# One matmul for the shared last query rows of a head pair, tails in one query block, and another order of the work

## The chip, the cores and the metric

One Trainium2 chip, one of its cores. The metric is the device time of one execution in microseconds, lower being better. Engines are named as in the profile: PE (TensorE), DVE (VectorE), ACT (ScalarE), POOL (GpSimd), and SP, the engine whose queue issues all DMAs of this kernel.

## What is computed

Attention with pooled queries, followed by a gated MLP with mixing along the sequence:

```python
# q, k, v: (4 batches, 8 heads, 1152, 64)
q_pool = q.reshape(B, H, 576, 2, D).mean(axis=3)
scores = q_pool @ k^T / sqrt(64);  scores -= max(scores, axis=-1)
attn = exp(scores) / (sum(exp(scores)) + 1e-9)
x = (attn @ v) with heads side by side              # (4, 576, 512)
h = gelu(x @ w_in);  u, v = halves of h             # 512 columns each
v = layernorm(v) * g_ln
v = w_sg @ v + b_sg                                 # mixing over 576 positions
out = x + (u * v) @ w_out
```

Inputs come as float32 and the weights and scores need more than half precision: the kernel splits most operands into a high and a low part of 16 bits and adds up the products.

## The kernel before, in words

The 32 heads are taken as 16 pairs p. A head has 576 pooled queries: four blocks of 128 rows and a last one of 64, the tail. Keys are 9 blocks of 128. For each pair:

- `load` (lines 338 to 352) brings in the raw keys, queries and values of two heads. POOL adds neighbouring queries (`pool`, lines 423 and 425), ACT and DVE make the high and low parts (`q_hi` L441, `q_lo` L445, `k_hi` L428, `k_lo` L431), and DMA transposes on SP write `q1` and `k1` (L449, L435). `k1` holds the high part of the keys in partitions 0 to 63 and the low part in 64 to 127; `q1` holds the high part of the queries twice. A plain DMA copies the upper half of `k1` into `k2` (L438).
- `maxima` (L499, L505) finds the largest score of each query row ahead of the real scores: per block of 128 query rows two matmuls of 512 key columns and one of 128, with a reduction on DVE after each bank. The rows are counted r = 0 to 8. r = 4 is the shared block: 64 tail rows of the first head in the lower half, 64 of the second in the upper half. Its queries are two zero-padded blocks of `q1` (4 and 5), one for each head, so each of its pieces takes two accumulating matmuls, one for each head's keys. After r = 4, and again after r = 8, DVE gathers the maxima (`done`, L529), POOL splits them (`split`, L535 to L537) into columns of `n2` beside the low parts of the queries, and a transpose DMA (`turn`, L540) writes `q2`. The first `turn` carries blocks 0 to 4, the second blocks 5 to 9.
- `attend` then goes over the key blocks j of head 0 and head 1. A main unit is two matmuls of 512 columns into a PSUM bank, `scores(0)` with `k1`, `q1` and `scores(1)` with `k2`, `q2` (L574), the exponential on ACT (L582), a high part on ACT (L588), a rest (L593) and matmuls with the values into `avp` (L602, or L609 for pairs 0 and 2, which keep float32). A tail unit does the same for the last 64 queries against several key blocks; it follows j = 4 and j = 8. The rest of a "kept" unit, half of the main units by `KEEP`, is made by DVE from PSUM; that of the others by POOL from SBUF. All `scores(0)` stay in program order (the marker `sseq`), and so do all matmuls into `avp`.

After 8 heads of a batch, `project` (through `unit`, L757) multiplies by `w_in`, and `gmlp` does the rest and stores. This work lies between the attention of the following batch; for the last batch it stands alone at the end.

Nothing of this is issued in the order of the code. Each step is given to `Schedule.add` with an engine, a duration, what it reads and writes, and a due time; `Schedule.run` simulates forwards and backwards `PASSES` times, shifts some due times by the seeds in `MOVES`, and the last forward run emits the instructions. An engine takes its instructions strictly in the order emitted. PSUM has 3 score banks (`S`), 3 banks `X`, 1 bank `M`, and `avp`. Maxima of pairs 4 and later use only `X`.

The wait on which much below rests, as the code has it:

```python
q1r = [f"q1{c}{hh}"] + ([f"q1{c}0"] if hh else [])
add("PE", ds, lambda: scores(0), r=[f"k1{c}{hh}", "clear"] + q1r, ...)
add("PE", ds, lambda: scores(1), r=[f"k2{c}{hh}", f"q2{c}{hh}", f"k2z{c}"], ...)
```

Of the kernel before, what the change touches and what calls it, by code (L numbers as in the profile page):

```python
# [222 lines left out]
def attention_gmlp_kernel(  # L223
# [57 lines left out]
    q2 = tiles(const, 2, [128, 10, 128], F16, "q2")  # L281
    mp = tiles(const, 2, [128, 9, 3], F32, "mp")
    qs = const.tile([128, 10, D], F32, name="qs")
    n1 = const.tile([128, 10, 2, D], F16, name="n1")
    n2 = const.tile([128, 10, 128], F16, name="n2")
# [87 lines left out]
    def scales(p, i, due):  # L373
# [36 lines left out]
        add("DVE", 0.64, power, r=[f"ps{p}{i}"], w=[st, f"pm{i}"], due=due, rel=[("x", "sc", p, i)])  # L410

    def prepare(p):
# [5 lines left out]
        for h in range(2):  # L418
            blk = slice(5 * h, 5 * h + 5)

            def pool(h=h):

                nc.gpsimd.tensor_tensor(out=qs[:, 6 * h:6 * h + 4, :], in0=qr[:, h, :, 0, :], in1=qr[:, h, :, 1, :], op=ALU.add)  # L423
                r = slice(64 * h, 64 * h + 64)
                nc.gpsimd.tensor_tensor(out=qs[r, 4 + h, :], in0=qe[r, 0, :], in1=qe[r, 1, :], op=ALU.add)
# [22 lines left out]
            def q_turn(blk=blk):  # L448
                nc.sync.dma_start_transpose(out=q1[c][:, blk], in_=n1[:, blk].rearrange("p i t d -> p (i t d)"))  # L449

            add("POOL", 0.97, pool, r=["qr"], w=[f"qs{h}"], due=t + lead("PL", p) + h)
            add("ACT", 0.72, q_hi, r=[f"qs{h}", sct], w=[f"n1{h}"], due=t + lead("QH", p) + h * HS[p > 0])
            add("SP", 0.7, q_turn, late=LATE[1] * (p > 0), issue=1.25, r=[f"n1{h}"], w=[f"q1{c}{h}"], due=t + lead("QH", p) + h * HS[p > 0])
# [4 lines left out]
            add("DVE", 0.46, q_lo, port=True, r=[f"qs{h}", sct, f"n1{h}"], w=[f"n2q{h}"], due=t + lead("QL", p) + h * HS[p > 0])  # L458
# [22 lines left out]
    def maxima(p):  # L481
# [5 lines left out]
        def rows(r):  # L487

            return ([(0, 4), (1, 5)], [0, 1]) if r == 4 else ([(0, r)], [0]) if r < 4 else ([(1, r + 1)], [1])

        def piece_of(group, j0, nj, g):
            nonlocal n
            r0, x = group[0][0], ("x", p, group[0][0], g)
# [16 lines left out]
            cols = w * sum(len(ops) for _, ops, _ in group)  # L510
            heads = sorted({h for _, _, hs in group for h in hs})
            add("PE", cols / 2400.0 + 0.003 * len(group), piece, r=[f"q1{c}{h}" for h in heads] + [f"k1{c}{h}" for h in heads], w=[x],
                due=due, acq=(x, where))
            add("DVE", w * len(group) / 960.0 + 0.07, top, r=[x], w=[f"mp{c}{a}{g}" for a, _, _ in group], due=due - 0.5, rel=[x])

        for r in range(9):
            ops, hs = rows(r)

            for g in range(2):
                piece_of([(r, ops, hs)], 4 * g, 4, g)  # L520
            if r in (3, 4, 8):
                piece_of([(a, *rows(a)) for a in {3: range(4), 4: (4,), 8: range(5, 9)}[r]], 8, 1, 2)
            if r in (4, 8):
                due = t + lead("X", p) + lead("XS", p) * n * 1.29 if p else -20 + n
                h = r // 8
                nm = nmx[h]

                def done(h=h, nm=nm):
# [725 lines left out]
```

## Time and profile before

| | |
|---|---|
| median of 3 runs | 638.8 us (638.28 to 639.22) |
| the profiled execution | 635.98 us, of which 634.2 us from first to last instruction |
| PE, DVE, ACT, POOL busy | 603.6, 528.5, 531.0, 380.8 us |
| granted TensorE clock, mean | 1.000 of 2.4 GHz |
| DMA | 71.49 MB, of the 16 engines' time 52% |

Busy time of PE runs from a matmul's start to its modelled end, and ends overlap with the starts of the next ones: a mean of one is longer than its share of the time. The warm-up matmuls at line 920 count as busy too. The time of an SP row is that of issuing a DMA; when it lands is a separate number.

### The profile page before, as it was taken

Reading aid. Unit: us, or ns where it says so; the run is one execution under the profiler, and the core shown is the slowest. Engines: PE = TensorE matmul, PEld = TensorE weight load, DVE = VectorE, ACT = ScalarE, POOL = GpSimd, SP = SyncE. Lnnn points to the kernel's source line nnn. Section 1 sums busy time; section 2 is a strip of 40 time slices with the busy share of each in tenths; the row PEclk is TensorE's granted clock in tenths of the full one; section 3 lists DMA queues with packets and bytes.
Section 4 is the critical chain, followed back from the end, with each engine's and each line's share of the span. In section 5 each row is a group of like instructions: output and inputs, shape, how many; then the busy total and the mean of one; then the engine's idle time right before and its main releaser. Section 6 shows DMA issues by size and latency. Waiting matters only on the chain.

```text
span 634.2 us, 18243 instructions
## 1 busy us (share of the span) xinstructions
PE 603.6 (95%) x7228; PEld 409.2 (65%) x7228; DVE 528.5 (83%) x1052; ACT 531.0 (84%) x987; POOL 380.8 (60%) x481
## 2 busy tenths in 40 slices
PE   5899899997999899999999999999999999999997
PEld 3387567864567566667566775676666775776755
DVE  4989899898989999999987999879998997753662
ACT  7478898799999989999999999798999988784420
POOL 8133375477556688855574677785475565962163
PEclk9999999999999999999999999999999999999999
DMA  9988961957655245568678334807772221141002
GB/s 262 236 209 217 185 135 39 198 121 121 129 115 121 61 79 133 111 136 177 114 160 181 35 51 94 154 24 193 132 170 52 68 41 20 12 84 36 26 1 74
DMA packets 129078, 71.49 MB, mean 113 GB/s; under 512 B 107424, under 2 KB 111520, under 8 KB 128864
## 3 DMA queue, kind: packets, MB, share of 16 engines
q1 hardware_dynamic: 128992, 70.33, 51.7%
q8 instruction: 56, 0.92, 0.6%
q14 instruction: 30, 0.25, 0.1%
HBM read 36.23 MB, written 4.72 MB: 65 GB/s over the span
## 4 chain that ended last, share of the span: by engine, by line
PE 64%; DVE 14%; ACT 5%; issue 1%; DMA 1%; POOL 0%; ACTq 0%; DVEq 0%; POOLq 0%
PE px L757 18%; PE s L574 14%; PE avp L602 13%; PE pm L757 7%; PE px L499 7%; DVE mp L505 5%; DVE f L593 2%; PE s L757 1%; ACT f L588 1%; PE avp L609 1%; ACT e L582 1%; DMA x<-in_moe_w_out_dram 1%; DVE n L445 1%; PE pm L857 1%; DVE dn L644 1%
## 5 line engine op out<-in xcount | busy, mean ns | idle before, releaser
L593 POOL TENSOR_TENSOR f<-e,f 128x512 f16<-128x512 f32 (+2 forms) x182 | 193.0, 1068 | 108.1 <-ACT f L588 93.0
L574 PE MATMUL s<-q,k 128*128 128x512 f16 (+1 forms) x1152 | 231.2, 286 | 12.8 <-ACT e L582 5.2
L505 DVE TENSOR_REDUCE mp<-px 128x1 f32<-128x512 f32 (+2 forms) x316 | 199.8, 663 | 18.1 <-PE px L499 16.2
L602 PEld LDWEIGHTS <-f 128*128 128x128 f16 x3780 | 150.4, 97 | 56.3 <-issue 10.6
L602 PE MATMUL avp<-va,f 128*128 128x65 f16 x3780 | 166.0, 193 | 1.5 <-POOL f L593 1.0
L582 ACT ACTIVATE e<-s 128x512 f32<-128x512 f32 (+2 forms) x226 | 124.9, 558 | 15.6 <-PE s L574 11.1
L499 PE MATMUL px<-k,q 128*128 128x512 f16 (+1 forms) x454 | 118.7, 325 | 2.1 <-DVE mp L505 1.6
L574 PEld LDWEIGHTS <-k 128*128 128x128 f16 x1152 | 82.6, 99 | 51.0 <-issue 15.6
L588 ACT ACTIVATE f<-e 128x512 f16<-128x512 f32 (+2 forms) x182 | 107.1, 591 | 4.5 <-issue 2.0
L593 DVE TENSOR_TENSOR f<-s,f 128x512 f16<-128x512 f32 x126 | 85.9, 682 | 22.7 <-ACT f L588 22.3
L582 ACT ACTIVATE s<-s 128x512 f32<-128x512 f32 x126 | 76.9, 611 | 8.1 <-PE s L574 7.5
L588 ACT ACTIVATE f<-s 128x512 f16<-128x512 f32 x126 | 77.4, 614 | 4.3 <-PE avp L602 2.4
L499 PEld LDWEIGHTS <-q 128*128 128x128 f16 x480 | 42.2, 99 | 27.0 <-issue 6.2
L609 PEld LDWEIGHTS avp<-va,e 128*128 128x128 f32 x360 | 46.1, 192 | 3.1
L609 PE MATMUL avp<-va,e 128*128 128x65 f32 x360 | 45.6, 270 | 0.0
L757 PE MATMUL px<-wsg,vz 128*128 128x512 f16 x168 | 43.6, 379 | 0.0
L423 POOL TENSOR_TENSOR qs<-qr 128x256 f32<-128x256 f32 x32 | 25.1, 786 | 22.3 <-DVE n L445 11.2
L757 PE MATMUL px<-wout_h,xg 128*128 128x512 f32 x100 | 38.2, 425 | 0.0
L757 PEld LDWEIGHTS <-win_h 128*128 128x128 f16 x320 | 30.0, 98 | 12.6 <-issue 1.0
L648 POOL TENSOR_TENSOR x<-a,dn 128x320 f32<-128x320 f32 x32 | 25.3, 789 | 17.2 <-DVE dn L645 13.2
L757 PE MATMUL px<-xt,win_h 128*128 128x288 f16 (+2 forms) x220 | 34.9, 262 | 0.0
L757 PEld LDWEIGHTS <-vz 128*128 128x128 f16 x224 | 20.5, 98 | 20.6 <-issue 0.4
(166 smaller groups left out, 1012.3 us busy)
## 6 DMA issues: line engine op xcount, KB each, us to landing
kr<-in_k_dram SPq DMA_DIRECT2D x16, 576.0 KB, 4.6
qr<-in_q_dram SPq DMA_DIRECT2D x16, 512.0 KB, 4.0
vr<-in_v_dram SPq DMA_DIRECT2D x14, 576.0 KB, 4.1
k<-k SPq DMA_DIRECT2D x32, 144.0 KB, 3.1
x<-in_moe_w_in_dram SPq DMA_DIRECT2D x8, 512.0 KB, 5.9
out_dram<-t SPq DMA_DIRECT2D x16, 256.0 KB, 2.3
x<-in_moe_w_out_dram SPq DMA_DIRECT2D x8, 256.0 KB, 3.5
u<-in_moe_w_sg_dram SPq DMA_DIRECT2D x1, 1152.0 KB, 7.0
```

The costliest lines, as they stand in the source:

```text
L423: nc.gpsimd.tensor_tensor(out=qs[:, 6 * h:6 * h + 4, :], in0=qr[:, h, :, 0, :], in1=qr[:, h, :, 1, :], op=ALU.add)
L445: nc.vector.scalar_tensor_tensor(out=n2[:, blk, 0:D], in0=qs[:, blk], scalar=s[:, 1:2], in1=n1[:, blk, 0, :], op0=ALU.mult, op1=ALU.subtract)
L499: nc.tensor.matmul(out=bank(x)[:, w * i:w * i + w], lhsT=q1[c][:, o, :], rhs=k1[c][:, h, j0:j0 + nj, :].rearrange("p j k -> p (j k)"), sta ...
L505: nc.vector.tensor_reduce(out=mp[c][:, r0:r0 + len(group), g], in_=src, axis=AX.X, op=ALU.max)
L574: nc.tensor.matmul(out=buf(("s", u))[:, col:col + w], lhsT=kk[c][:, hh, j, :], rhs=qq[:, o:o + w], start=(i == 0 and m == 0), stop=(i == 1 ...
L582: nc.scalar.activation(out=s if kept else buf(("e", u))[:, 0:n], in_=s, func=AF.Exp, scale=SCALE * 2.0**-ASH)
L588: nc.scalar.activation(out=buf(("f", u))[:, 0, 0:n], in_=exponentials(), func=AF.Copy)
L593: eng.tensor_tensor(out=f[:, 1, 0:n], in0=exponentials(), in1=f[:, 0, 0:n], op=ALU.subtract)
L602: nc.tensor.matmul(out=avp[:, o:o + m], lhsT=w[:, col:col + 128], rhs=vv, start=(j == 0 and k == 0 and not tail and x == 0), stop=(j == KJ ...
L609: nc.tensor.matmul(out=avp[:, o:o + D + 1], lhsT=e[:, col:col + 128], rhs=vw[c][:, KJ * hh + j, :], start=(j == 0 and k == 0 and not tail) ...
L648: nc.gpsimd.tensor_tensor(out=xbuf[b % 2][:, :, col], in0=a[:, :, 0:D], in1=d.rearrange("p (i o) -> p i o", o=1).to_broadcast([128, 5, D]) ...
L757: nc.tensor.matmul(out=bank(m)[:, o[0] if o else slice(0, cols)], lhsT=l, rhs=r, start=(k + j == 0), stop=(k + j == n - 1), skip_group_che ...
```

## The change

The shared block r = 4 becomes one matmul per piece. A tenth block of `n1` gets the first head's tail queries in the first 64 columns of the first 64 rows and the second head's in the other corner, zeros elsewhere; after the transpose that is a block-diagonal query block (`q1` block 9). A new tile `kx` holds the high parts of both heads' keys, one above the other; two new DMAs per pair copy them from `k1`. The product has the high parts of the keys alone, for the maxima of these 128 rows. Tail queries of both heads now lie in one block 4, which belongs to the second half of each step: POOL adds them in one instruction of 128 rows, the first half has blocks 0 to 3, the second blocks 4 to 8 (9 for `q1`). The first `done`/`split`/`turn` now comes after r = 3. The tail units of both heads read the second half's `q1` and `q2`.

Beside that: `KEEP` goes from 0.5 to 0.53, first chunks of `project` wait for `wn0`, `wn1`, and in the last batch its first three units use only banks `X` and `M` and wait for the last maxima, the others for the last head's output; planner durations, `PASSES` and `MOVES` are new, so the whole order is.

```diff
-    q2 = tiles(const, 2, [128, 10, 128], F16, "q2")
+    q2 = tiles(const, 2, [128, 9, 128], F16, "q2")
+    kx = const.tile([128, KJ, 128], F16, name="kx")
...
-            blk = slice(5 * h, 5 * h + 5)
+            blk = slice(4, 9) if h else slice(0, 4)
+            n = 4 + h
...
-                nc.gpsimd.tensor_tensor(out=qs[:, 6 * h:6 * h + 4, :], in0=qr[:, h, :, 0, :], in1=qr[:, h, :, 1, :], op=ALU.add)
-                r = slice(64 * h, 64 * h + 64)
-                nc.gpsimd.tensor_tensor(out=qs[r, 4 + h, :], in0=qe[r, 0, :], in1=qe[r, 1, :], op=ALU.add)
+                nc.gpsimd.tensor_tensor(out=qs[:, 5 * h:5 * h + 4, :], in0=qr[:, h, :, 0, :], in1=qr[:, h, :, 1, :], op=ALU.add)
+                if h:
+                    nc.gpsimd.tensor_tensor(out=qs[:, 4, :], in0=qe[:, 0, :], in1=qe[:, 1, :], op=ALU.add)
+
+            def q_cross():
+
+                for a in range(2):
+                    r = slice(64 * a, 64 * a + 64)
+                    nc.gpsimd.tensor_copy(n1[r, 9, a, :], n1[r, 4, a, :])
+
+            def k_cross(h=h):
+                nc.sync.dma_start(out=kx[64 * h:64 * h + 64], in_=k1[c][0:64, h])
...
-            def q_turn(blk=blk):
+            def q_turn(blk=slice(4, 10) if h else blk):
                 nc.sync.dma_start_transpose(out=q1[c][:, blk], in_=n1[:, blk].rearrange("p i t d -> p (i t d)"))
...
-            return ([(0, 4), (1, 5)], [0, 1]) if r == 4 else ([(0, r)], [0]) if r < 4 else ([(1, r + 1)], [1])
+            if r == 4:
+                return q1[c][:, 9, :], kx, [f"q1{c}1", "kx0", "kx1"]
+            return q1[c][:, r, :], k1[c][:, r // 4 if r < 4 else 1], [f"q1{c}{r // 5}", f"k1{c}{r // 5}"]
...
-                for i, (_, ops, _) in enumerate(group):
-                    for k, (h, o) in enumerate(ops):
-                        nc.tensor.matmul(out=bank(x)[:, w * i:w * i + w], lhsT=q1[c][:, o, :],
-                                         rhs=k1[c][:, h, j0:j0 + nj, :].rearrange("p j k -> p (j k)"), start=(k == 0),
-                                         stop=(k == len(ops) - 1))
+                for i, r in enumerate(group):
+                    qb, kb, _ = rows(r)
+                    nc.tensor.matmul(out=bank(x)[:, w * i:w * i + w], lhsT=qb, rhs=kb[:, j0:j0 + nj, :].rearrange("p j k -> p (j k)"),
+                                     start=True, stop=True)
...
-            if r in (4, 8):
+            if r in (3, 8):
...
-        o = (704 if hh else TM) if tail else 768 * hh
+        o = TM + TT * hh if tail else 640 * hh
+        qh = 1 if tail else hh
...
-        q1r = [f"q1{c}{hh}"] + ([f"q1{c}0"] if hh else [])
+        q1r = [f"q1{c}{qh}"]
...
-        add("PE", ds, lambda: scores(1), r=[f"k2{c}{hh}", f"q2{c}{hh}", f"k2z{c}"], w=[f"s{u}"], due=g - 0.7)
+        add("PE", ds, lambda: scores(1), r=[f"k2{c}{hh}", f"q2{c}{qh}", f"k2z{c}"], w=[f"s{u}"], due=g - 0.7)
...
-        ready = [f"xt{ct}" for ct in range(CT if b < B - 1 else CT - 1)]
+        last = b == B - 1
+        ready = ["wn0", "wn1"] + [f"xt{ct}" for ct in range(CT - last)]
+        early = ready + (["nm0", "nm1"] if last else [])
+        if last:
+            ready = ready + [f"x{b % 2}{H - 1}"]
...
-KEEP = (0.5, 0.5)
+KEEP = (0.53, 0.53)
...
-PASSES = 14
+PASSES = 7
```

`MOVES` goes from 76 seeds to 100 other ones.

## Rows read from the trace of the kernel before

**Rows 1.** The page, parts 1 and 4: busy time, and the last chain by engine.
```profile
PE 603.6 (95%) x7228; PEld 409.2 (65%) x7228; DVE 528.5 (83%) x1052; ACT 531.0 (84%) x987; POOL 380.8 (60%) x481
PE 64%; DVE 14%; ACT 5%; issue 1%; DMA 1%; POOL 0%; ACTq 0%; DVEq 0%; POOLq 0%
```

**Rows 2.** Three stretches: length, busy by engine (instructions), granted clock, DMA share, GB/s.
```profile
20.00:160.00 140.00, 128.62 (x1412) 94.05 (x1411) 129.03 (x271) 116.27 (x232) 70.76 (x100) 1.00 0.75 160
160.00:560.00 400.00, 393.46 (x5137) 261.22 (x5136) 354.79 (x692) 372.22 (x689) 267.80 (x331) 1.00 0.50 103
560.00:634.20 74.20, 70.13 (x625) 47.36 (x624) 34.19 (x63) 27.13 (x45) 28.96 (x28) 1.00 0.14 38
```

**Rows 3.** PE and weight loads in the first of these, for line 920 (warm-up) alone.
```profile
20.00:160.00 140.00, 7.45 (x22) 2.11 (x22) 1.00 0.75 160
```

**Rows 4.** PE in order of time: runs of maxima matmuls, four each (start, length, count).
```profile
520.98 1.03 PE L499 MATMUL px<-k,q 128*128 128x512 f16 x4
515.13 0.39 PE L499 MATMUL px<-k,q 128*128 128x128 f16 x4
```

**Rows 5.** Weight loads of the maxima, all pairs (count, ns min/median/max).
```profile
L499 PEld LDWEIGHTS <-q x480: 95/98/153, 18.2 to 552.2; 128*128 128x128 f16 x160
```

**Rows 6.** DVE, groups by line and shape (count, busy us, mean ns, idle before).
```profile
L505 DVE TENSOR_REDUCE mp<-px 128x1 f32<-128x512 f32 x271 | 177.0, 680 | 17.1 <-PE px L499 15.4 <-PE px L396 0.6
L593 DVE TENSOR_TENSOR f<-s,f 128x512 f16<-128x512 f32 x126 | 85.9, 682 | 22.7 <-ACT f L588 22.3
L445 DVE SCALAR_TENSOR_TENSOR n<-qs,sc,n 128x320 f16<-128x320 f32 x32 | 21.9, 691 | 0.6 <-DMA q<-n 0.4
```

**Rows 7.** POOL and ACT, the same view.
```profile
L593 POOL TENSOR_TENSOR f<-e,f 128x512 f16<-128x512 f32 x126 | 150.2, 1193 | 88.9 <-ACT f L588 75.9 <-PE s L574 3.3 <-PE px L499 3.2
L425 POOL TENSOR_TENSOR qs<-qe 64x64 f32<-64x64 f32 x32 | 11.4, 357 | 1.3
L536 POOL CAST n<-nm 128x5 f16<-128x5 f32 x32 | 7.6, 239 | 2.2
L441 ACT ACTIVATE n<-qs,sc 128x640 f16<-128x640 f32 x32 | 26.9, 841 | 2.0 <-POOL qs L425 2.0
```

**Rows 8.** DMA of line 438: all of them (KB, us to landing), and two issues on SP.
```profile
k<-k SPq DMA_DIRECT2D x32, 144.0 KB, 3.1
42.79 1.13 SPq L438 DMA_DIRECT2D k<-k  x2
```

**Rows 9.** Pair 0: first two reductions, second gathering, second `turn`, first tail's `scores(1)`.
```profile
18.99 1.28 DVE L505 TENSOR_REDUCE mp<-px 128x1 f32<-128x512 f32 x2
36.69 0.16 DVE L529 TENSOR_REDUCE nm<-mp 128x5 f32<-128x15 f32 x1
40.89 1.23 SPq L540 DMA_TRANSPOSE q<-n  x1
35.88 0.53 PE L574 MATMUL s<-q,k 128*128 128x64 f16 x6
```

**Rows 10.** Line 540, all `turn`s: from issue to landing.
```profile
DMA to landing us min/median/max: 2.6/2.9/6.9
```

**Rows 11.** Pair 15: its second `turn` and the first tail's `scores(1)`.
```profile
555.96 1.24 SPq L540 DMA_TRANSPOSE q<-n  x1
553.03 0.31 PE L574 MATMUL s<-q,k 128*128 128x64 f16 x5
```

**Rows 12.** Waits of PE (engine, line, for what: us, times, longest).
```profile
PE s L574 <- ACT e L582: 5.2, 12, 1.2
PE s L574 <- DVE f L593: 4.2, 8, 1.0
PE s L574 <- DMA q<-n: 2.5, 1, 2.5
```

**Rows 13.** The last head's end: ACT empties `avp`, POOL norms, ACT takes up `xn`.
```profile
578.92 0.44 ACT L641 ACTIVATE a<-avp 128x325 f32<-128x325 f32 x1 [2.87 <-PE avp L602]
580.75 0.83 ACT L681 ACTIVATE xn<-x,xs 128x640 f16<-128x640 f32 x1 [1.39 <-POOL x L648]
```

More of the change, by code (lines that the diff above doesn't have):

```diff
@@ L446, in q_lo @@
                                                op0=ALU.mult, op1=ALU.subtract)
[L448 removed]
+            def q_turn(blk=slice(4, 10) if h else blk):
                 nc.sync.dma_start_transpose(out=q1[c][:, blk], in_=n1[:, blk].rearrange("p i t d -> p (i t d)"))
[L451 to L453 removed]
+            add("POOL", 1.15 if h else 0.8, pool, r=["qr"], w=[f"qs{h}"], due=t + lead("PL", p) + h)
+            add("ACT", 0.72 if h else 0.6, q_hi, r=[f"qs{h}", sct], w=[f"n1{h}"], due=t + lead("QH", p) + h * HS[p > 0])
+            if h:
+                add("POOL", 0.45, q_cross, r=["n11"], w=["n1x"], due=t + lead("QH", p) + h * HS[p > 0])
+            add("SP", 0.85 if h else 0.6, q_turn, late=LATE[1] * (p > 0), issue=1.25, r=[f"n1{h}"] + ["n1x"] * h, w=[f"q1{c}{h}"], due=t + lead("QH", p) + h * HS[p > 0])
             add("ACT", 0.67, k_hi, r=["kr", sct], w=[f"kh{h}"], due=t + lead("KH", p) + h * HS[p > 0])
@@ L457, in prepare @@
             add("SP", 0.41, k_copy, late=LATE[1] * (p > 0), r=[f"k1{c}{h}"], w=[f"k2{c}{h}"], due=t + lead("KC", p) + h * HS[p > 0])
-            add("DVE", 0.46, q_lo, port=True, r=[f"qs{h}", sct, f"n1{h}"], w=[f"n2q{h}"], due=t + lead("QL", p) + h * HS[p > 0])
+            add("SP", 0.41, k_cross, late=LATE[1] * (p > 0), r=[f"k1{c}{h}"], w=[f"kx{h}"], due=t + lead("KC", p) + h * HS[p > 0])
+            add("DVE", 0.46 if h else 0.4, q_lo, port=True, r=[f"qs{h}", sct, f"n1{h}"], w=[f"n2q{h}"], due=t + lead("QL", p) + h * HS[p > 0])
     def values(p):
@@ L509, in piece_of @@
             where = (["X", "M", "S"] if r0 < 4 else ["X", "M"]) if p == 0 else ["X", "M"] if p < NP else XB
[L510 to L514, printed above, removed]
+            cols = w * len(group)
@@ L516, in maxima @@
+            add("PE", cols / 2400.0 + 0.003 * len(group), piece, r=sorted({a for r in group for a in rows(r)[2]}), w=[x], due=due,
+                acq=(x, where))
+            add("DVE", w * len(group) / 960.0 + 0.07, top, r=[x], w=[f"mp{c}{a}{g}" for a in group], due=due - 0.5, rel=[x])
         for r in range(9):
-            ops, hs = rows(r)
             for g in range(2):
-                piece_of([(r, ops, hs)], 4 * g, 4, g)
+                piece_of([r], 4 * g, 4, g)
             if r in (3, 4, 8):
-                piece_of([(a, *rows(a)) for a in {3: range(4), 4: (4,), 8: range(5, 9)}[r]], 8, 1, 2)
@@ L535, in split @@
                     nc.gpsimd.tensor_scalar(out=nm, in0=nm, scalar1=1.0 / MW, scalar2=None, op0=ALU.mult)
                     nc.gpsimd.tensor_copy(hi, nm)
-                    nc.gpsimd.tensor_tensor(out=n2[:, 5 * h:5 * h + 5, D + 1], in0=nm, in1=hi, op=ALU.subtract)
-                def turn(h=h):
-                    nc.sync.dma_start_transpose(out=q2[c][:, 5 * h:5 * h + 5, :], in_=n2[:, 5 * h:5 * h + 5, :].rearrange("p i c -> p (i c)"))
-                add("DVE", 0.17, done, r=[f"mp{c}{a}{g}" for a in range(4 * h, 4 * h + 5) for g in range(3)], w=[f"nm{h}"], due=due - 0.5)
+                    nc.gpsimd.tensor_tensor(out=n2[:, blk, D + 1], in0=nm, in1=hi, op=ALU.subtract)
@@ L543, in maxima, with turn @@
+                def turn(blk=blk):
+                    nc.sync.dma_start_transpose(out=q2[c][:, blk, :], in_=n2[:, blk, :].rearrange("p i c -> p (i c)"))
+                add("DVE", 0.17, done, r=[f"mp{c}{a}{g}" for a in range(blk.start, blk.stop) for g in range(3)], w=[f"nm{h}"], due=due - 0.5)
                 add("POOL", 0.76, split, r=[], w=[f"nm{h}", f"n2m{h}"], due=due - 0.5)
-                add("SP", 0.7, turn, late=LATE[2] * (p > 0), issue=1.25, r=[f"n2q{h}", f"n2m{h}"], w=[f"q2{c}{h}"], due=due - 1)
+                add("SP", 0.7 if h else 0.6, turn, late=LATE[2] * (p > 0), issue=1.25, r=[f"n2q{h}", f"n2m{h}"], w=[f"q2{c}{h}"], due=due - 1)
```

32 lines of the change are left out of this document (17 added, 15 removed), and 19 rows, old and new, of the table MOVES.

## The prediction

> **What bounds the kernel now.** I read the page's busy times first, then the chain that ended last, then a table by stretches, because a share over the whole span mixes stages with different limits. PE is busy 95% of the span, DVE 83%, ACT 84%, and PE holds 64% of the last chain against 14% for DVE [rows 1]. The stretches say where that holds [rows 2]. From 160 to 560 us PE is busy 393.46 of 400 us, with ACT at 372.22 and DVE at 354.79: here only 6.5 us of PE are empty, and work taken from PE is time. From 20 to 160 us it is otherwise: DVE is busy 129.03 of 140 us and PE 128.62, of which 7.45 are warm-up matmuls that compute nothing [rows 3]. DVE sets the pace there, PE follows. From 560 us the gated MLP of the last batch stands alone on PE; the change takes nothing from that. The granted clock is 1.00 in all three, so every matmul is priced at 2.4 GHz.
>
> **What one matmul is worth.** The busy time of a matmul contains its way through the array, which overlaps with the next. So I take the distance between starts: four maxima matmuls of 512 columns in a row last 1.03 us. One alone shows 0.38, so the three further ones add (1.03 - 0.38) / 3 = 0.217 us each; four of 128 columns last 0.39 us, the three further ones about 0.056 each [rows 4].
> The Trainium skill has a rule that makes less of this: the page "TensorE: Matmul & The Clock Gate", section "Back-to-back issue gap", puts the sustained spacing of matmuls of 512 columns in a real kernel at about 131 ns and of 128 columns at 81 ns, and calls 216 ns the spacing of an isolated one. By that, as an estimate, the removed work would be 32 x 0.131 + 16 x 0.081 = 5.5 us. The trace does not agree with it here.
>
> **The change, part by part.**
>
> *Removed from PE.* r = 4 took 6 matmuls a pair, now 3: two of 512 columns and one of 128 fewer, 2 x 0.217 + 0.056 = 0.49 us a pair, 7.8 us over 16. Their weight loads go from 480 to 432 [rows 5]; they overlap. No matmul is added. Pairs 0 to 4 have their maxima before 160 us, pairs 5 to 15 after. The later eleven give 11 x 0.49 = 5.4 us, taken in full since PE is the limit there. The earlier five hold 2.4 us; DVE is the limit or nearly so, and the number of reductions on DVE does not change (21 a pair, 0.68 us each [rows 6]), so the gain lies between 0 and 2.4. PE and DVE are equally busy there, so I take half, 1.2.
>
> *The tails' new wait.* This is the change's price. A first tail's `scores(1)` now needs the second `turn` of its pair, so all maxima of both heads. Today it does not, and the trace shows how late that `turn` is: in pair 0 it is issued at 40.89 us and lands 2.9 us later, while the tail's matmuls ran at 35.88, 7.9 us before that [rows 9, 10]; in pair 15 it is issued at 555.96, the tail ran at 553.03, 5.8 us before landing [rows 11, 10]. Worked out so for every pair, landing comes after the tail in 12 of 16, by 0.4 to 8.9 us, 64 us in sum. Behind the waiting matmul stand all later scores (they keep their order), so ACT's exponentials too, and the matmuls into `avp` behind these. An order laid out for the new dependency can start the maxima of each pair that much earlier: they run during the pair before, their buffers `k1`, `q1` come in twos, and the amount of work is the same, so after pair 0 the lead need be won only once. Bounds: 0 to 64 us; I take 0 past pair 0, because that lead is at most a quarter of the 37 us or so that a pair lasts (16 pairs in some 580 us).
>
> *Pair 0* can't be moved ahead of its loads. Its first `turn` comes sooner: r = 4 is no longer before it, three reductions fewer, two at 0.60 us (two in a row last 1.28, one 0.68 [rows 6, 9]) and a short one, about 1.4 us; PE waits 2.5 us for it now [rows 12]. Its second gathering stands at 36.69 [rows 9], with work for pair 1 and for the weights among its reductions on DVE. They began at 18.99. If the rest steps back, 21 reductions of 0.60 end at about 31.6 us, and with the 4.2 us from gathering to issue (40.89 - 36.69, a bound) or 1.5 at best (my estimate for three small POOL instructions of 0.24 and the hand-over), and 2.9 to land, `q2` is there at 36 to 38.7, where the tail runs now. So between -1.4 (a gain) and +7.9 us; near the first, since DVE's order can be changed freely: I take 0.
>
> *Two more copies a pair on SP.* The nearest row is the copy of `k1` into `k2`, of the same shape: 144 KB, 3.1 us to landing, 0.57 us to issue [rows 8]. 32 of them are 18 us of issuing over the span. They stand behind the same landing as the `k2` copies, so SP waits for nothing new; what is queued behind (transposes, loads, stores) goes out 0.6 to 1.2 us later. r = 4 gets its keys about 3.7 us later than now, but it can be taken last among its pair's maxima. Cover: the lead of the maxima. I take 0; if it is used up in pair 0, 1.2 us; DMA traffic is 0.75 busy in 20 to 160 us and 0.50 after [rows 2], so room is there.
>
> *POOL.* One addition fewer a pair (0.357), two small copies more. The trace has no copy of 64 by 64: 0.239 (a cast of 128x5) to 0.357 (an addition of that shape) [rows 7], so 16 x (0.12 to 0.36) = +2 to +6 us. `KEEP` hands 8 of 252 units to DVE (134 kept instead of 126), -8 x 1.193 = -9.5. POOL is busy 267.80 of 400, and waits for ACT before its residuals; nothing on the path, 0. The copies stand between `q_hi` and the second `q_turn`, half a microsecond of lead.
>
> *DVE and ACT.* DVE gets 8 x 0.682 = +5.5 us of rests, and saves at most a fifth of 0.691 in 16 `q_lo`s, -2.2; ACT saves at most a fifth of 0.841 in 16 `q_hi`s, -2.7 [rows 6, 7]. A kept unit holds a score bank longer: PE waits 4.2 us for DVE over 126 of them [rows 12], so 8 more are +0.3 us.
>
> *End.* V units may start only when the last maxima are done, the later ones and U when the last head is written. From emptying `avp` to `xn` is 580.75 - 578.92 = 1.8 us [rows 13]; three V units of 9 matmuls that need no last head (27 x 0.217 = 5.9 us) cover it. 0; without that cover 1.8 us.
>
> *The new order* by itself moves every stall. PE's empty time is 6.5 us in the long stretch and 11.4 in the early one. It can go either way: I take 0, with bounds of about a third of that, 6 us, on both sides.
>
> **Sum**, against the profiled execution of 635.98 us (634.2 of span and 1.8 around it): -5.4 - 1.2 + 0.3 = -6.3, so 629.7. The median of the runs stands 2.8 us above that execution; I carry this over: 632.5 us.
>
> **Rivals.**
> *A better order* (rival 1): PE's empty time shrinks by a third as well, -6.3 - 6 = -12.3, so about 626.5. For it: stalls of PE are many and short, with no single cause [rows 12]. Against it: PE is already at 98% in the long stretch.
> *The cover is DVE's* (rival 2): the early stretch gives nothing, and DVE, with 3 us more work and 89% busy after 160 us, keeps half of the 5.4: -2.7 + 0.3 = -2.4, 636.4, up to 639 if pair 0's wait is paid as well.
> *The tails wait* (rival 3, slower): maxima of the second head can't be drawn ahead, since the three `X` banks are shared with the MLP and DVE is nearly full, so the first tail of each pair stands waiting for `q2`. 64 us are at stake; from 6.3 / 16 = 0.4 us a pair it eats the gain. A quarter of it left is 16 us, so 638.8 - 6.3 + 16 = 648.5.
> *The change does not do what it says*: if removed matmuls were cheap because PE is waiting anyway, that is rival 2; by the count of matmuls there is no doubt that they go.
>
> **How the numbers follow.** Forecast (628.5 to 636.5): 0.58. Rival 1 (below 628.5): 0.13. Rival 2 (636.5 to 640): 0.15. Rival 3 (above 640): 0.14. About 0.2%, 1.3 us, is what a measurement of this kernel can tell from no change: from 637.5 to 640.1 counts as same. Faster: forecast, rival 1 and a third of rival 2, 0.58 + 0.13 + 0.05 = 0.76; same 0.10; slower 0.14. The range takes in rival 1's value and rival 2, and leaves out most of rival 3: 626 to 640.5.
>
> **What would show each step.** Weight loads of the maxima 432 instead of 480, and PE's busy time down by about 8 us; in 160 to 560 us the same work done in about 5 us less. The second `turn` of each pair landing before its first tail, and PE's waits of scores for the DMA into `q` staying near 2.5 us: if they grow to tens of microseconds, rival 3 is true. If PE's busy share falls below 95% with DVE's above 85%, rival 2 is. The forecast is wrong if the order's stalls, which no row of before can show, change by more than the removed work.

## The result and the profile after

The changed kernel takes 643.36 us (median of 5 runs, 641.25 to 646.7) against 638.5 (5 runs, 635.6 to 639.22): ratio 1.0097, interval [1.0072, 1.0123]. It is slower, by 4.9 us of the medians or 6.2 by the ratio; 632.5 was forecast, and the range ended at 640.5. The profiled execution took 642.94 us, 641.2 of it span, 7.0 more than before's.

The removed work did go. These are the page of after (busy time, chain by engine) and the weight loads of the maxima, answering to [rows 1, 5]:

```profile
PE 601.9 (94%) x7180; PEld 406.5 (63%) x7180; DVE 535.1 (83%) x1060; ACT 530.0 (83%) x987; POOL 373.5 (58%) x489
PE 29%; DVE 10%; ACT 3%; issue 1%; DMA 0%; POOL 0%; DVEq 0%; POOLq 0%
L515 PEld LDWEIGHTS <-q x432: 95/98/153, 19.7 to 549.7; 128*128 128x128 f16 x144
```

The chain of after can be followed back over 43% of the span only, so its shares are not to be set beside before's. 48 weight loads of the maxima are gone, 480 to 432, and PE has 48 matmuls fewer, 7228 to 7180. Yet its busy time fell only by 1.7 us, and its span grew. Part of the rest is a stretch at half the clock, shown below, in which PE was busy 5.67 of 6.8 us, about twice as long as the same work takes at the full clock (an estimate from 1.2 against 2.4 GHz). Where the time went is best seen by batches, cut where the last head of each batch leaves `avp`. Columns: length, then busy time of PE, PEld, DVE, ACT, POOL (instructions), granted clock, DMA share, GB/s. Before:

```profile
0.00:155.12 155.12, 136.95 (x1437) 99.03 (x1437) 134.71 (x290) 126.77 (x245) 80.93 (x120) 1.00 0.77 171
155.12:299.75 144.63, 139.46 (x1821) 92.28 (x1821) 134.34 (x261) 138.40 (x262) 100.90 (x124) 1.00 0.56 120
299.75:438.48 138.73, 136.20 (x1813) 90.57 (x1811) 122.92 (x238) 128.91 (x239) 93.56 (x115) 1.00 0.53 110
438.48:578.92 140.44, 139.83 (x1827) 93.42 (x1826) 109.69 (x214) 123.90 (x231) 87.00 (x105) 1.00 0.36 73
578.92:634.20 55.28, 51.21 (x337) 33.95 (x335) 26.84 (x52) 13.02 (x15) 18.45 (x17) 1.00 0.13 39
```

And after:

```profile
0.00:159.32 159.32, 139.06 (x1431) 98.28 (x1432) 140.17 (x302) 131.12 (x256) 79.66 (x125) 1.00 0.82 187
159.32:306.13 146.81, 139.51 (x1808) 92.48 (x1805) 133.53 (x257) 133.50 (x251) 99.68 (x129) 0.98 0.50 109
306.13:449.24 143.11, 138.38 (x1821) 92.67 (x1820) 129.59 (x248) 131.92 (x245) 91.68 (x118) 1.00 0.60 124
449.24:585.57 136.33, 134.15 (x1793) 89.96 (x1792) 104.91 (x205) 120.42 (x225) 83.63 (x102) 1.00 0.34 76
585.57:641.20 55.63, 50.80 (x334) 33.09 (x332) 26.93 (x51) 13.03 (x15) 18.88 (x17) 0.99 0.12 35
```

Take PE's busy time from each length. PE stood empty for 18.2, 5.2, 2.5, 0.6 and 4.1 us before, and for 20.3, 7.3, 4.7, 2.2 and 4.8 us after: 8.7 us more in all, 1.6 to 2.2 in each of the four batches and 0.8 at the end, no single place. That, less the 1.7 us of busy time, is the 7.0 us of span. Single batches are longer and shorter by up to 4 us besides, because maxima and MLP work lie in other batches than before; only the sum counts.

The second thing stands in the granted clock of batch 1, 0.98. The fall lies between 160 and 180 us; three stretches of 10 us:

```profile
150.00:160.00 10.00, 9.58 (x143) 6.10 (x139) 9.97 (x20) 9.86 (x22) 6.15 (x9) 1.00 0.64 129
160.00:170.00 10.00, 6.70 (x76) 3.94 (x73) 8.95 (x20) 7.74 (x16) 4.63 (x5) 0.77 0.51 109
170.00:180.00 10.00, 10.00 (x123) 6.37 (x122) 8.75 (x16) 8.60 (x18) 7.31 (x10) 0.89 0.19 42
```

PE's instructions there, with the idle time before each and who ended it:

```profile
161.86 0.38 PE L515 MATMUL px<-k,q 128*128 128x512 f16 x1
162.99 0.59 PE L588 MATMUL s<-q,k 128*128 128x512 f16 x2 [0.75 <-ACT e L596]
164.99 0.64 PE L588 MATMUL s<-q,k 128*128 128x512 f16 x2 [1.41 <-ACT e L596]
166.76 0.59 PE L588 MATMUL s<-q,k 128*128 128x512 f16 x1 [1.14 <-DVE f L607]
167.14 0.63 PE L515 MATMUL px<-k,q 128*128 128x512 f16 x1
```

PE waits three times, 0.75 to 1.41 us, for score banks: ACT and DVE are making the high and low parts of `x` of the batch just ended. From 165.4 to 172.2 us the granted clock is at 1.2 instead of 2.4 GHz, and the maxima matmul at 167.14 takes 0.63 us, where the one at 161.86 took 0.38. The fall came 0.4 us after the second wait had ended; the third lies within the slow stretch. The profile of before has no such stretch [rows 2]. The mean granted clock of after's five runs is 0.989 to 0.997, with 0.992 in the middle; of 65 runs of before, taken beside the experiments, the middle one has 0.997 (median time 637.5 us), and only 16 have 1.000 like the profiled one. So after's trace stands beside an execution of before that lost nothing to the clock.

PE's waits after, for [rows 12], and last a line of before for the third of them:

```profile
PE s L588 <- ACT e L596: 8.5, 13, 1.4
PE s L588 <- DVE f L607: 5.2, 6, 1.6
PE px L515 <- DVE mp L520: 4.9, 11, 1.3
PE px L515 <- DMA kx<-k: 1.1, 1, 1.1
PE px L499 <- DVE mp L505: 1.6, 5, 0.7
```

Waits for ACT are 8.5 us instead of 5.2, for DVE's rests 5.2 instead of 4.2, of the maxima for DVE 4.9 instead of 1.6. The wait of a score for the DMA into `q`, 2.5 us before, is gone altogether.

### The profile page after: what moved, and what is told of

It is laid out like the page before. It is cut to its first block, busy times and chain, and to the rows that moved or that the text cites. A ratio compares the mean times of both kernels' runs of the same rounds, so it can differ in the third digit from the quotient of the medians.

```text
span 641.2 us, 18254 instructions
## 1 busy us (share of the span) xinstructions
PE 601.9 (94%) x7180; PEld 406.5 (63%) x7180; DVE 535.1 (83%) x1060; ACT 530.0 (83%) x987; POOL 373.5 (58%) x489
## 5 line engine op out<-in xcount | busy, mean ns | idle before, releaser
L607 POOL TENSOR_TENSOR f<-e,f 128x512 f16<-128x512 f32 (+2 forms) x174 | 184.8, 1068 | 127.4 <-ACT f L602 108.0
L596 ACT ACTIVATE e<-s 128x512 f32<-128x512 f32 (+2 forms) x218 | 119.5, 552 | 15.9 <-PE s L588 14.7
L607 DVE TENSOR_TENSOR f<-s,f 128x512 f16<-128x512 f32 x134 | 91.2, 682 | 33.8 <-ACT f L602 31.3
L602 ACT ACTIVATE f<-e 128x512 f16<-128x512 f32 (+2 forms) x174 | 101.5, 584 | 6.1 <-PE avp L616 2.7
L515 PE MATMUL px<-k,q 128*128 128x512 f16 (+1 forms) x366 | 98.3, 325 | 6.4 <-DVE mp L520 3.7
L515 PEld LDWEIGHTS <-q 128*128 128x128 f16 x432 | 38.1, 98 | 30.9 <-issue 12.0
L775 PE MATMUL px<-wout_h,xg 128*128 128x512 f32 x116 | 44.2, 425 | 0.0
L775 PE MATMUL px<-win_h,xt 128*128 128x512 f16 x112 | 41.4, 379 | 1.0 <-DVE mp L520 1.0
L775 PEld LDWEIGHTS <-xt 128*128 128x128 f16 x224 | 19.9, 98 | 20.2 <-issue 1.9
L439 ACT ACTIVATE kn<-kr,sc 128x576 f16<-128x576 f32 x32 | 24.7, 787 | 9.4 <-DVE sc L406 7.5
```

Source lines behind the costliest of these rows:

```text
L439: nc.scalar.activation(out=kn[:, h, :, 0, :], in_=kr[:, h], func=AF.Copy, scale=s[:, 0:1])
L515: nc.tensor.matmul(out=bank(x)[:, w * i:w * i + w], lhsT=qb, rhs=kb[:, j0:j0 + nj, :].rearrange("p j k -> p (j k)"), start=True, stop=True)
L596: nc.scalar.activation(out=s if kept else buf(("e", u))[:, 0:n], in_=s, func=AF.Exp, scale=SCALE * 2.0**-ASH)
L602: nc.scalar.activation(out=buf(("f", u))[:, 0, 0:n], in_=exponentials(), func=AF.Copy)
L607: eng.tensor_tensor(out=f[:, 1, 0:n], in0=exponentials(), in1=f[:, 0, 0:n], op=ALU.subtract)
L775: nc.tensor.matmul(out=bank(m)[:, o[0] if o else slice(0, cols)], lhsT=l, rhs=r, start=(k + j == 0), stop=(k + j == n - 1), skip_group_che ...
```

## The experiments

Beside each stand its median, the ratio to the runs of before taken beside it, with the 95% interval, and what follows. Before took 637.4 to 638.1 us in these. Theory A: PE's work is time, and the loss is elsewhere. Theory B: PE's work was covered by the other engines. Theory C: the new order costs, whatever is in it. Theory D: the tails wait for the second `turn`.

### What the removed matmuls are worth

**e1_joint_old_order**: the shared block as one matmul, the order of before kept instruction by instruction. Tails lie in a block of the first half; two small ACT copies a pair write the corners.

```diff
+                    if len(ops) == 2:
+                        nc.tensor.matmul(out=bank(x)[:, w * i:w * i + w], lhsT=q1[c][:, 5, :],
+                                         rhs=kx[:, j0:j0 + nj, :].rearrange("p j k -> p (j k)"), start=True, stop=True)
+                        continue
```

> The kernel before in its own order, with the shared row alone changed: one matmul of block-diagonal queries and kx per piece, 32 more DMAs for kx put where the keys' transposes land, the two corner blocks made by two small ACT copies a pair. Tails of both heads lie in one block of the first half, so no tail waits longer than before. Theory 'order' (removed PE work is worth its time; the new order loses it): 631 to 634 us, 5 to 7 us under the kernel before. Theory 'cover' (PE waits for DVE and ACT anyway): within 2 us of before, 637 to 640. Theory 'tails' (the wait of the tails is the price): as theory 'order' here, since the tails' wait is not in it.

651.26 us, 1.0212 [1.0176, 1.0248]. Its waits of PE:

```profile
PE px L529 <- DMA kx<-k: 6.6, 1, 6.6
PE s L612 <- ACT e L620: 11.4, 19, 1.3
```

In pair 0 PE stood 6.6 us for `kx`, and the clock was at half from 28.2 to 35.0 us, and later twice for 3.4 us; ACT had 10 us more to do. Three effects at once, so it prices none of them.

**e5_before_drop** does it alone: the kernel before, the second head's keys left out of the shared block, nothing moved.

```diff
-                    for k, (h, o) in enumerate(ops):
+                    for k, (h, o) in enumerate(ops[:1]):
...
-                                         stop=(k == len(ops) - 1))
+                                         stop=True)
```

> The kernel before in its own order with nothing changed but the second of the two accumulating matmuls of the shared row left out (the maxima of the second head's last 64 rows are then not computed, so those rows are shifted by another value). This takes exactly the 7.8 us of PE work out that the change takes out, with no new DMA, copy, wait or order. Theory 'order' (removed matmuls are worth their time): 630 to 633 us, 5 to 7.5 us under before. Theory 'cover' (PE waits for DVE and ACT anyway): under 3 us of gain, 635 to 638.

636.36 us, 0.9977 [0.9954, 0.9999]. 7.8 us of PE's work went and the time fell by 1.0 (medians) to 1.5 us (ratio). The same cut by batches, from an execution of 638.42 us, the longest of the ten:

```profile
0.00:156.56 156.56, 136.34 (x1421) 98.62 (x1424) 133.69 (x290) 126.90 (x245) 80.54 (x120) 0.99 0.77 170
156.56:301.49 144.93, 139.40 (x1809) 92.06 (x1807) 134.76 (x261) 138.66 (x261) 101.00 (x124) 0.99 0.58 118
301.49:441.12 139.63, 135.11 (x1800) 89.70 (x1799) 123.12 (x238) 128.83 (x239) 94.07 (x115) 1.00 0.53 111
441.12:581.36 140.24, 138.87 (x1817) 92.58 (x1816) 109.52 (x214) 123.92 (x230) 87.00 (x105) 1.00 0.36 73
```

PE is empty for 20.2, 5.5, 4.5 and 1.4 us of these (before 18.2, 5.2, 2.5, 0.6): 5.1 us of what is taken from PE come back as waiting. Its waits of scores for ACT rise from 5.2 to 7.1 us, for the DMA into `q` from 2.5 to 4.0 [rows 12]. Theory A falls for this order.

```profile
PE s L574 <- ACT e L582: 7.1, 14, 1.2
PE s L574 <- DMA q<-n: 4.0, 3, 2.5
79.74 0.38 PE L574 MATMUL s<-q,k 128*128 128x512 f16 x1 [2.51 <-DMA q<-n]
81.20:84.60 3.40, 3.40 (x28) 1.75 (x25) 2.83 (x4) 2.97 (x6) 3.13 (x5) 0.50 0.58 201
```

The last two lines tell why this execution is so long: after a wait of 2.51 us, which the profile of before has too without any fall, the clock stood at half for 3.4 us, and once more from 159.7 to 163.1 us. The gain of 1.0 to 1.5 us is read from the medians, at the same middle clock of 0.997 as before's.

**e9_before_extra** adds as much: a third matmul in each piece of the shared block.

```diff
-                    for k, (h, o) in enumerate(ops):
+                    for k, (h, o) in enumerate(ops + ops[1:] if len(ops) == 2 else ops):
```

> The kernel before in its own order with one matmul more per piece of the shared row instead of one fewer (the second head's scores are added twice, so its last 64 rows are shifted by another value): +7.8 us of PE work. Taking as much out gave 1.0 us. If PE is simply not the limit of this order: within 2 us of before, 636 to 639.5. If the order is laid out to the work it has, so that work put in costs and work taken out is not missed: +4 to +7 us, 641 to 645, as in the changed kernel's order, where the same work put back cost 5.2.

644.43 us, 1.0121 [1.0094, 1.0149]: 7.8 us more of PE cost 7.0. So the order of before lies at a corner: work added to PE is time nearly in full, work taken from it is not.

**e10_drop_and_less_dve** and **e11_drop_and_less_act** ask whose limit holds e5: the same removal, with less on DVE (reductions of the shared block over half the columns, expected -8.5 us) or less on ACT (sums of squares over 10 of 18 groups, expected -13 us).

```diff
+                if r0 == 4 and g < 2:
+                    src = src[:, :, 0:256]
```
```diff
-            src = src.rearrange("p h j d -> p (h j) d")
+            src = src.rearrange("p h j d -> p (h j) d")[:, 0:10]
```

> As the kernel with the second matmul left out, and the reductions of the shared row over 256 of 512 columns (the maxima of that row miss half of the keys): PE -7.8 us and, by 0.27 us for each of 32 reductions, DVE -8.5 us. If DVE is what hides the removed PE work: 629 to 633. If not: 635 to 637, as without this.

> As the kernel with the second matmul left out, and the sums of squares behind the scales of keys and values over 10 of 18 column groups (the scales come out a little larger): PE -7.8 us and, by about 0.43 us for each of 30, ACT -13 us. If ACT is what hides the removed PE work: 628 to 633. If not: 635 to 637.

634.96 us, 0.9974 [0.9945, 1.0003], and 633.6, 0.9944 [0.9928, 0.9961]. Busy times of e5, e10 and e11:

```profile
PE 600.9 (94%) x7178; PEld 406.9 (64%) x7180; DVE 527.9 (83%) x1052; ACT 531.3 (83%) x987; POOL 381.0 (60%) x481
PE 600.8 (95%) x7180; PEld 407.1 (64%) x7180; DVE 523.9 (82%) x1052; ACT 530.8 (84%) x987; POOL 379.6 (60%) x481
PE 600.4 (95%) x7180; PEld 407.4 (64%) x7180; DVE 529.7 (84%) x1052; ACT 520.0 (82%) x987; POOL 381.8 (60%) x481
```

DVE's busy time fell by 4.0 us from e5 to e10, not by the 8.5 expected, and ACT's by 11.3 from e5 to e11. With less on ACT the gain is 3.8 us instead of 1.0; with less on DVE it is 2.4 by the medians, which can't be told from e5 by the intervals. Since far less was taken off DVE, the two runs don't say which engine is the larger part of the cover; nor was before run with less on ACT or DVE alone. In both, not half of PE's work comes out: the three engines are all close to the limit.

**e2_after_extra_matmuls** puts the work back into the changed kernel, each matmul of the shared block issued twice.

```diff
+                    if r == 4:
+                        nc.tensor.matmul(out=bank(x)[:, w * i:w * i + w], lhsT=qb, rhs=kb[:, j0:j0 + nj, :].rearrange("p j k -> p (j k)"),
+                                         start=True, stop=True)
```

> The changed kernel with the removed PE work put back in the same order: each matmul of the shared row is issued twice into the same place. Theory 'order': the 48 matmuls cost again what they took, +5 to +8 us, 648 to 651. Theory 'cover': +0 to +2 us, 643 to 645. Theory 'tails': +5 to +8.

648.63 us, 1.0175 [1.0152, 1.0197]: 5.3 us over after. In after's order the removal is worth 5.3 us, close to what the forecast had; with the same matmuls as before that order lies 11 us above before's. Its page beside before's [rows 1], with as many matmuls, has PE empty for 37.7 of 646.2 us instead of 30.6 of 634.2, 7.1 us more, and busy 4.9 us longer; in two stretches of about 3.4 us its clock was at half.

```profile
PE 608.5 (94%) x7226; PEld 410.8 (64%) x7228; DVE 535.3 (83%) x1060; ACT 530.9 (82%) x987; POOL 373.5 (58%) x489
```

**e6_before_halves** and **e7_after_halves** compute the shared block another way, without `kx`: two matmuls of 64 weight columns into the two halves of the partitions, in before and in after's order (there without the 32 DMAs and the corner copies).

```diff
+                        for h, o in ops:
+                            r = slice(64 * h, 64 * h + 64)
+                            nc.tensor.matmul(out=bank(x)[r, w * i:w * i + w], lhsT=q1[c][:, o, r],
+                                             rhs=k1[c][:, h, j0:j0 + nj, :].rearrange("p j k -> p (j k)"), start=True, stop=True)
+                        continue
```

> The kernel before in its own order, the shared row by two matmuls of 64 weight columns each, one into the upper and one into the lower half of the bank's partitions, instead of two accumulating ones of 128 columns. If the two run beside each other in the array, PE work falls by 7.8 us as with the changed kernel's single matmul and without its DMAs and copies: the same time as with the second matmul left out. If they run one after the other: the time of before, 636 to 639.

> The changed kernel in its order, with the shared row by the same two half matmuls on k1 and the common tail block: no kx, none of its 32 DMAs, no corner copies on POOL, and PE's 1.1 us wait for kx in pair 0 gone. If these additions cost nothing but that wait: 641 to 643 us if the halves run beside each other. If SP's queue pays for the 32 DMAs as well: 636 to 640. If the halves run one after the other: 5 us more than either.

638.95 us, 1.0013 [0.999, 1.0036], and 648.97, 1.0185 [1.0155, 1.0214]. PE in e7:

```profile
198.79 0.41 PE L515 MATMUL px<-k,q 128*64 128x512 f16 x2
199.13 0.60 PE L592 MATMUL s<-q,k 128*128 128x512 f16 x2
200.75 0.25 PE L515 MATMUL px<-k,q 128*64 128x128 f16 x2
200.93 0.39 PE L592 MATMUL s<-q,k 128*128 128x512 f16 x1
```

From two halves of 512 columns to the next matmul it is 0.34 us, of 128 columns 0.18: a pair's shared block takes 2 x 0.34 + 0.18 = 0.86 us, against 0.98 for two accumulating matmuls a piece and 0.49 for one. So e6 takes 1.9 us from PE, which before's order does not show, and e7 puts 5.9 back, which after's order shows as 5.6. And since e7 has none of the `kx` DMAs and copies and is no better than e2, these cost nothing that the two runs can tell, with intervals of 1.4 to 1.9 us either way.

### The clock

**e3_after_filled**: the changed kernel with 8, 16 and 13 small matmuls (184 columns, into unused columns of `avp`'s bank, where they disturb the running sum of one head) ahead of the three waiting scores.

```diff
+            if not tail:
+                for _ in range({156: 8, 158: 16, 160: 13}.get(count[0], 0)):
+                    nc.tensor.matmul(out=avp[:, 328:512], lhsT=unit_b[:, 0:128], rhs=unit_b[:, 0:184], start=True, stop=True)
+                count[0] += 1
```

> The changed kernel with 37 matmuls of 184 columns into unused columns of the accumulator's bank, ahead of the three score matmuls that wait 0.75, 1.41 and 1.14 us at 163 to 167 us, where the granted clock then stood at half for 6.8 us. If that clock is what parts its runs (five times of 641.3 to 646.7 us at mean granted clocks of 0.997 to 0.989): 638 to 641 us, clock 0.998 or more. If the clock at half there costs nothing, because PE is waiting anyway: 643 or more, with the clock restored.

640.14 us (10 runs), 1.0042 [1.0024, 1.0061], 3.2 us below after, by adding work. The two stretches that had 0.77 and 0.89:

```profile
160.00:170.00 10.00, 9.57 (x129) 7.02 (x128) 9.80 (x22) 8.62 (x18) 5.72 (x6) 1.00 0.57 116
170.00:180.00 10.00, 10.00 (x132) 6.16 (x131) 9.72 (x17) 9.62 (x20) 6.98 (x9) 1.00 0.16 41
```

The fall there is gone (this execution has another, of 3.4 us at 85.3 us, where after's has none), and so is half of the loss. It fits the clock of the runs: 0.992 against 0.997 is 0.5% of 640 us, 3.2 us; the intervals leave some 2 us either way. The traces of e2, e7 and e12, which keep after's order and its three waits, have the fall too, at 169.1, 167.3 and 167.5 us.

### The start, the tails and the order

**e12_after_start**: pair 0's first reductions, gathering and `turn` moved ahead in the changed kernel; the gathering at 27.1 us instead of 29.16.

```diff
+SWAPS = ((84, 111), (77, 102), (85, 102), (92, 102), (121, 240))
```

> The changed kernel in its order but for pair 0's start: on DVE the three reductions of later rows that stand ahead of the first gathering come after it (on PE one matmul accordingly), and on SP the second turn goes ahead of two transposes for pair 1. The first gathering comes 2.5 us sooner, at about 26.5 us. If the later start of the attention (23.4 instead of 20.9 us at the first score, 2.5 to 3.4 us behind through the first five pairs) is a lasting loss: 640 to 641.5, 2 to 3 us under the changed kernel. If it is won back anyway: 643 to 644.

643.54 us, 1.0104 [1.0087, 1.012]. No gain, so the late first gathering isn't what costs. But the attention did not start sooner by it: the first score stands at 24.13 us, in after at 23.42, before at 20.92, and head 0 leaves `avp` at 53.29, 52.54 and 50.06 us. What the late start itself costs is not shown.

**e15_tails_first_half**: tails and shared block in the first half, so that no tail depends on the second `turn`; an order laid out for that.

```diff
-            blk = slice(4, 9) if h else slice(0, 4)
-            n = 4 + h
+            blk = slice(5, 9) if h else slice(0, 5)
+            n = 5 - h
...
-            if r in (3, 8):
+            if r in (4, 8):
```

> The changed kernel with its one matmul for the shared row, kx and everything else, but with the tails' block and the shared row in the first half (as in the kernel before, the first turn carries blocks 0 to 4 and both heads' tails need that alone), in an order found in the same way. Theory 'tails': with the wait gone it lies with the kernel before, 634 to 640. Theory 'order': anywhere from 637 to 655, as the changed kernel's other orders.

655.15 us, 1.0264 [1.0211, 1.0318]: worse without the dependency. The order changed with it, so the time alone decides little. Theory D, taken as PE waiting for the second `turn`, falls because after's trace has no such wait.

The others lay out orders anew with the kernel's own planner and other seeds, for before's operations (e8, e13), after's (e4, e14), and before's with one of the small edits: `KEEP` (e16), durations and waits of the last batch (e18); e17 is after without the `KEEP` edit. `MOVES` has 110 seeds in after (not 100, as said above) and 76 in before; these orders and e15's have 13 to 47.

```diff
-MOVES = ((773038, 0), (875599, 2), ...
+MOVES = ((140891, 0), (567712, 0), ...
```
```diff
-KEEP = (0.5, 0.5)
+KEEP = (0.53, 0.53)
```
```diff
-        add("DVE", 0.64, power, r=[f"ps{p}{i}"], w=[st, f"pm{i}"], due=due, rel=[("x", "sc", p, i)])
+        add("DVE", 0.26 if i else 0.39, power, r=[f"ps{p}{i}"], w=[st, f"pm{i}"], due=due, rel=[("x", "sc", p, i)])
```

> The operations of the kernel before, unchanged, in another order (other MOVES and PASSES, nothing else), found in the same way as the other order of the changed kernel's operations, which took 656 us (650.6 to 659.2). Theory 'order': this one too lands several us above before, 645 to 660, so that an order is worth more than the removed work. Theory 'tails': the changed operations alone take badly to an order; this stays at 636 to 643.

> The operations of the kernel before in a third order (other MOVES and PASSES). Its first two took 637.4 and 639.9 us. If its operations lie well in many orders: 636 to 643. If orders differ by chance alone: anything up to 655.

> The changed kernel's operations in another order (other MOVES and PASSES, nothing else). Theory 'order': another order lands elsewhere, several us away on either side, 632 to 648, and a good one shows the removed work, under 637. Theory 'tails': every order of these operations stays at 641 or above.

> The changed operations in a third order, found in the same way as that of the kernel before's. The first two took 643.4 and 656.4 us. Theory 'tails' (maxima of both heads are needed before the first tail, which costs in any order): 643 or more. Theory 'order': as like to be under 640 as over 650.

> The operations of the kernel before with KEEP at 0.53 alone (8 more rests on DVE and 8 fewer on POOL), in an order found in the same way. If KEEP is what the changed kernel suffers from: 645 or more. If not: 637 to 643, as the other orders of these operations.

> The changed kernel with KEEP back at 0.5 (nothing else), in an order found in the same way. If KEEP is the cause: 637 to 643. If the shared row with kx, or the smaller edits, are: 645 to 657, as its other orders.

> The operations of the kernel before with the change's smaller edits alone: the shorter planner durations of the scale step, project's first chunks waiting for wn0, wn1 and in the last batch for the last maxima and the last head, the spatial transposes waiting for wsc; KEEP 0.5, shared row and tails as before; in an order found in the same way. If these edits are the cause: 645 or more. If not: 637 to 643.

The table sets the medians beside the middle run's mean granted clock. The last column is the middle one of the products of time and clock, run by run: what would be left if each half-clock stretch had been pure loss, so the most that the clock can explain.

| | us | ratio | clock | us x clock |
|---|---|---|---|---|
| before (65 runs) | 637.5 | 1 | 0.997 | 636.0 |
| e8, before's operations | 639.92 | 1.0051 [1.0031, 1.0071] | 0.997 | 638.3 |
| e13, before's operations | 641.66 | 1.0063 [1.0041, 1.0086] | 0.996 | 638.2 |
| after | 643.36 | 1.0097 [1.0072, 1.0123] | 0.992 | 639.3 |
| e4, after's operations | 656.41 | 1.028 [1.0222, 1.0339] | 0.981 | 642.7 |
| e14, after's operations | 652.95 | 1.0229 [1.0204, 1.0253] | 0.993 | 647.2 |
| e16, before with `KEEP` 0.53 | 650.56 | 1.0197 [1.0168, 1.0226] | 0.984 | 640.1 |
| e17, after with `KEEP` 0.5 | 650.35 | 1.0193 [1.012, 1.0266] | 0.990 | 641.5 |
| e18, before with the small edits | 648.12 | 1.0154 [1.0118, 1.0189] | 0.997 | 646.0 |

New orders cost 2 to 4 us for before's own operations and 5 to 19 for the edited ones. The clock can be half or more of that in e4, e16 and e17, and nearly nothing in e18. Fewer seeds don't explain the spread by themselves: e13 with 14 lies at 641.66 us, e4 with 13 at 656.41. Where e16 lost the clock, two stretches from its trace:

```profile
30.00:40.00 10.00, 7.41 (x30) 5.01 (x30) 8.94 (x15) 4.93 (x9) 4.17 (x5) 0.61 0.63 144
40.00:50.00 10.00, 10.00 (x50) 7.68 (x48) 3.76 (x9) 4.71 (x9) 2.93 (x6) 0.53 0.81 220
```

By the clock at most 0.39 x 10 + 0.47 x 10 = 8.6 us are lost in the two. In orders e4 and e14 the tails' wait does come up, as the DMA into `q`:

```profile
PE s L588 <- DMA q<-n: 9.8, 5, 4.3
PE s L588 <- DMA q<-n: 7.8, 6, 2.3
```

The first line is e4's, the second e14's. Of these, 6.5 and 5.1 us stand ahead of tails, the rest ahead of main units. So the dependency can cost; after's order avoids it. What makes e18 and e14 some 10 us slower apart from the clock stays open: all that they share beside a new order is the small edits, which after, e4 and e17 have too, and the orders were not taken apart step by step.

## Why the prediction was wrong, point by point

- *Removed from PE, -5.4 "taken in full since PE is the limit there", and -1.2.* The count was right (48 matmuls, 7.8 us). What they are worth depends on the order: e5 measured 1.0 to 1.5 us in before's, e2 5.3 in after's, not far from the 6.6 of the sum. The step failed where PE's 98% in the long stretch was read as "only PE counts". ACT at 93% and DVE at 89% [rows 2] hold PE's banks, all three go through their instructions in the order emitted, and in e5 a PE that runs ahead waits for them a little later. The bound was to be found in e5 and e9: -1.0 against +7.0 for the same 7.8 us. Rival 2 named the mechanism, with DVE as the cover and half of the gain left; in before's order less than a quarter of the 6.6 is left, and e10 and e11 leave open whether DVE or ACT covers more.
- *The new order, 0 (bounds of 6 us either way).* This is the step that made the kernel slower, and it lies outside its bound in both ways of counting: after stands 7.0 us above e5 (643.36 against 636.36), or, for the same matmuls, 11 us above before (e2), of which its lighter PE gets 5.3 back. Of this 3.2 us is the half clock at 165 us (e3), which the prediction didn't have, since it took the clock as 1.00 for good. The rest is PE standing empty: in the trace 3.6 us longer than in e5's, 1.8 of it in batch 1, whose three waits at 162 to 167 us hold 3.3. That this comes from the order as a whole is argued from the spread of e4 to e18, not shown piece by piece; `KEEP`, the smaller edits and what the order pays for drawing maxima ahead were not parted from it.
- *The tails' wait, 0 past pair 0; rival 3.* Right. In the trace after, the first tail's `scores(1)` follows the landing of the second `turn` in all 16 pairs, by 0.04 to 7.8 us, and PE stands idle for that DMA in none. The maxima were drawn ahead, as the prediction said they could be. (Before's 64 us were worked out with the median time to landing; with each `turn`'s own they are 68, in the same 12 pairs.) The time came out on rival 3's side for another reason.
- *Pair 0, 0 (-1.4 to +7.9).* Its second `turn` was issued at 38.33 us, where 33.1 to 35.8 was worked out, and the tail ran at 42.05 instead of 35.88 [rows 9]: +6, inside the bound. Head 0 left `avp` 2.5 us late; e12 shows that an earlier first gathering does not change that. One reading was wrong: PE's wait of 2.5 us for the DMA into `q` [rows 12] was put down to pair 0's first `turn`, but the trace of before has it at 78.47 us (last line), when the second `turn` of pair 1 had landed.

```profile
29.16 0.15 DVE L542 TENSOR_REDUCE nm<-mp 128x4 f32<-128x12 f32 x1
38.33 1.27 SPq L553 DMA_TRANSPOSE q<-n  x1
42.05 0.31 PE L588 MATMUL s<-q,k 128*128 128x64 f16 x5
78.47 0.38 PE L574 MATMUL s<-q,k 128*128 128x512 f16 x1 [2.46 <-DMA q<-n]
```

- *Two more copies a pair, 0.* Right as far as e7 against e2 can tell. In after's trace they take longer to land than their model row [rows 8], and that row takes 4.1 us instead of 3.1, but the lead of the maxima covers it; PE waited for `kx` once, 1.1 us.

```profile
kx<-k SPq DMA_DIRECT2D x32, 144.0 KB, 3.8
k<-k SPq DMA_DIRECT2D x32, 144.0 KB, 4.1
```

- *POOL, +2 to +6 and -9.5.* The corner copies take 0.290 us each, 9.3 in all, less 5.7 for the additions that went: +3.6. POOL's busy time fell by 7.3 (380.8 to 373.5), nothing of it on the path as far as the chain is followed.

```profile
L433 POOL COPY n<-n 64x64 f16<-64x64 f16 x32 | 9.3, 290 | 15.0 <-ACT n L452 14.0
L427 POOL TENSOR_TENSOR qs<-qe 128x64 f32<-128x64 f32 x16 | 5.7, 354 | 0.0
```

- *`KEEP`, +0.3.* PE's waits for DVE's rests rose by 1.0 us, 4.2 to 5.2, and DVE's busy time by 6.6 instead of about 3. Small, of the right sign; e16 and e17 can't give a price for it, since their orders differ.
- *End, 0.* Right within what shows: 55.28 us from the last head to the end before, 55.63 after.
- *The rule on the spacing of matmuls.* By the page "TensorE: Matmul & The Clock Gate", section "Back-to-back issue gap" of the Trainium skill, as an estimate, the removed work would have been 5.5 us. The sum went by 7.8. The starts in the trace, 0.217 us apart [rows 4], speak for 7.8. In time the same number of matmuls cost 7.0 us in e9 and 5.3 in e2, so the times alone don't decide between the two. The failing was not in the price of a matmul but in taking it for time.

The sum with measured terms, against before's 637.5: -1.0 to -1.5 for the removal in its old order, +3.2 for the clock, and some 4 us left for the order with the small edits. Only the first two were measured alone.

## What to carry to other kernels

When several engines that work strictly in order are all near 90%, the busy share of one of them does not price work taken from it: leave the work out once, and add it once, before you count on it. A re-laid order is a change of its own, here 2 to 19 us, and has to be costed with bounds taken from other orders of the same operations. Look at the granted clock wherever PE is left short for some microseconds, and in more than one execution: filling three waits of about 1 us with useless matmuls won 3.2 us.

## What was not expected of the hardware

- The granted clock fell to half for 6.8 us in after, 0.4 us after the second of two waits of 0.75 and 1.41 us had ended. A wait alone doesn't decide it: after one of 2.5 us the profile of before has no fall, while e5 and e9, in the same order, fell for 3.4 us after the same wait (2.51 and 2.09 us there).
- Two matmuls of 64 weight columns into separate halves of the partitions overlap in the records (two in 0.41 us), but the next matmul starts 0.34 us after the first, against 0.43 for two full ones: far from half. With 128 columns it is 0.18, against 0.11 for two full ones.
- The copies of 144 KB into `k2` landed in 3.1 us in before and 4.1 in after, which has twice as many such copies. The number is not what sets it: with as many as after, e12 has 3.3 and e4 2.7.
